# Third tile of x requested by SyncE ahead of V's weights, and a longer run of dummy matmuls ahead of the first V matmul

## The chip, the cores and the metric

The kernel runs on one core of one Trainium2 chip. The metric is the device time of one execution, in microseconds (us). The core's engines work side by side, each on its own queue of instructions in order: TensorE (PE in the profile; its weight loads are PEld), VectorE (DVE), ScalarE (ACT), GpSimd (POOL) and SyncE (SP). In this kernel SP does nothing but request transfers, and ACT requests some between its arithmetic. A request occupies the engine that makes it; the bytes are then moved by 16 DMA engines that all queues share.

## The reference

One input x of 2048 rows by 576 is normalized per row, and the normalized rows go through an attention with 32 heads of 18 and a sliding window of 256, and through a gated feed-forward layer of width 4608. Both results are added to x.

```python
xn = layernorm(x)                       # mean, variance per row, eps 1e-5
q, k, v = split(xn @ wqkv)              # 576 x 1728, 32 heads of 18
p = softmax(where(0 <= i - j < 256, q k^T * 18**-0.5, -1e9))
A = (p @ v) @ wo
B = (silu(xn @ w1) * (xn @ w3)) @ w2    # 576 x 4608, 4608 x 576
out = x + A + B
```

All tensors are bf16.

## The kernel before

The rows are handled in four chunks of 512 (`CH`), each of four tiles of 128 rows. A list of operations is built in program order by `add(engine, ...)`; afterwards `resolve` works out which semaphore waits each needs from the buffers that it reads and writes, and every engine replays its own operations in the order in which they were added. So the order of the calls is the order of every queue, and a DMA request sits in the queue of the engine that it was added to.

A chunk consists of the projections to Q, K and V (`proj_begin`, `proj_end`, `proj_part`), then 36 units of the feed-forward layer's first product (`unit_pairs`, line 768) with the attention's scores (630) and products with V (698) spread among them, and then the second product together with the output projection (`p2_mm`, line 839). Most matmuls come in pairs: one on the upper 64 rows of the TensorE array and one on the lower 64, each with its own bank of PSUM.

The change concerns the start of the first chunk, before the matrix work is under way. In program order:

- `load_x(t, eng)` (line 306) requests tile t of x, 128 x 576, into the buffer `xp`. The loop at lines 894 and 895 requests tile 0 on SP and tiles 1, 2 and 3 on ACT. Below, x0 to x3 are these tiles.
- ACT then loads an activation table (896), and SP requests V's weights: `wv` for the first 512 rows (897), then two pieces for the last 64 rows (901, "the tail of wv").
- SP goes on with the weights of Q and K into a buffer that lies in `pt` (927 and 931); POOL deals them into the tile `wp` in the order in which the projections read them (`deal`, 952).
- TensorE starts with dummy matmuls on a constant (921): three with 512 columns and 56 with 64 columns. Nothing reads their results. Two more follow behind the statistics of tile 0 (`warm`, 909).
- Layer norm of tile 0: statistics on DVE (396, 399), the square root on ACT (369), its reciprocal on DVE (374), the normalization on DVE (414). Tile 1 takes its statistics on ACT (387, 390). Tiles 2 and 3 take theirs on DVE, and the statistics of tile 2's first half stand in DVE's queue between the normalization of tile 0 and the reciprocal for tile 1.
- `xn_turn` transposes a normalized tile on TensorE (429), and ACT copies the result into `xnT` (442, 448).
- `warm_halves` (915) then issues one dummy pair on the two row halves with 256 columns into the banks that the first V projection will use, and `proj_begin(0, ("v", 0))` issues that projection: 288-column matmuls (500) with a tile of `xnT` standing and `wv` moving. Tiles 1 to 3 follow in the same manner, and the Q and K projections after them (also line 500, 512 columns, with `wp` standing).

Of the kernel before, what the change touches and what calls it, by code (L numbers as in the profile page):

```python
# [44 lines left out]
class _Prog:  # L45
# [13 lines left out]
    def add(self, eng, fn, r=(), w=(), j=(), dma=None, after=()):  # L59
        deps = []  # L60
        for k in r:
            deps += self.bufs[k].writers
        for k in w:
            g = self.bufs.get(k)
            if g is not None:
                deps += g.ahead(eng)
        for k in j:
            g = self.bufs[k].before
            if g is not None:
                deps += g.ahead(eng)  # L70
        op = _Op(eng, fn, deps + list(after), dma)
        op.after = tuple(after)
        self.n[eng] += 1
        op.pos = self.n[eng]
        if dma is not None:
            self.dma_count[dma] = self.dma_count.get(dma, 0) + 16
            op.cnt = self.dma_count[dma]
        for k in r:
            self.bufs[k].readers.append(op)
        for k in w:  # L80
            self.bufs[k] = _Gen([op], self.bufs.get(k))
        for k in j:
            self.bufs[k].writers.append(op)
        for k in w:
            if self.bufs[k].before is not None:
                self.bufs[k].before.before = None
        self.ops.append(op)
        return op
# [76 lines left out]
def bass_parallel_sum__sliding_block__glu_gated_swiglu__prompt_kernel(  # L165
# [17 lines left out]
    CH = 512  # L183
# [14 lines left out]
    with ExitStack() as es:  # L198

        def sb(name, shape, dtype=dt.bfloat16):  # L200
            return es.enter_context(nc.sbuf_tensor(name, shape, dtype))
# [66 lines left out]
        oq = sb("oq", [128, CH])  # L268
# [9 lines left out]
        PS = es.enter_context(nc.psum_tensor("ps", [128, 8, 512], dt.float32))  # L278
        JOBS, SC = ((0, 1), (2, 3), (4, 5)), (6, 7)
# [22 lines left out]
        def load_x(t, eng="sp"):  # L302
            nonlocal xp_ctr
            s = xp_ctr % NXP
            xp_ctr += 1
            add(eng, lambda e: e.dma_start(xp[s][:], x2[t * 128:(t + 1) * 128, :]), w=[("xp", s)], dma=f"xp{s}")
            return s
# [228 lines left out]
        def proj_begin(c, what, banks=None):  # L536
            banks = banks or job()
            last = proj_part(c, what, banks, 0)
            got = proj_end()
            pend.append((c, what, banks, last))  # L540
            return got
# [350 lines left out]

        xslot = {}
        for t in range(TB):
            xslot[t] = load_x(t, "act" if t else "sp")
        add("act", lambda e: e.preload_act_table_set("sqrt_and_others"))
        add("sp", lambda e: e.dma_start(
            wv[:, 0:4, :], A_wqkv[0:512, 2 * D:3 * D].rearrange("(kd p) f -> p kd f", p=128)),
# [10 lines left out]
                add("pe", lambda e, n=n: e.matmul(PS[:, b, 0:n], oq[:, 0:128], oq[:, 0:n], start=True, stop=True),  # L909
                    r=["oq0"], after=after, **{"j" if k else "w": [("ps", b)]})  # L910

        def warm_halves(banks):
            for r in range(2):
                rows = slice(64 * r, 64 * r + 64)
                add("pe", lambda e, b=banks[r], rows=rows, r=r: e.matmul(
                    PS[:, b, 0:256], oq[rows, 0:128], oq[rows, 0:256], start=True, stop=True, tile_position=(64 * r, 0)),
                    r=["oq0"], w=[("ps", banks[r])])

        ones = nc.const_aps.tensor(1.0, (128, CH), dt.bfloat16)
        for k, n in enumerate([CH] * 3 + [64] * 56):  # L920
            add("pe", lambda e, n=n: e.matmul(PS[:, 4, 0:n], ones[:, 0:128], ones[:, 0:n], start=True, stop=True),
                **{"j" if k else "w": [("ps", 4)]})

# [45 lines left out]
        ln_recip(0)  # L969
        ln_apply(0, xslot[0], (0, 2))  # L970
        xn_turn(0, (SC, JOBS[1]), ("act", "act"), spread=True)()
        warm_halves(JOBS[0])
        proj_begin(0, ("v", 0))
        ln_stats(2, xslot[2], 0)
        ln_recip(1)
# [72 lines left out]
        for c in range(NC):  # L1048
# [13 lines left out]
            start = START[c]  # L1062
# [119 lines left out]
            for u in range(NF):  # L1182
# [31 lines left out]
                if u in stat:  # L1214
                    t = (c + 1) * TB + stat[u]
# [4 lines left out]
                if u in apply:  # L1220
                    t = (c + 1) * TB + apply[u]
# [5 lines left out]
                if c == 0 and u == 13:  # L1227
                    for t in range(4):
                        r0 = 4 * Dh + 252 * (t // 2)
                        rows = A_wo[r0:r0 + 252, :].rearrange("(s p d) f -> p s d f", p=2, d=Dh)[t % 2, :, :, :]  # L1230
                        add("sp", lambda e, t=t, rows=rows: e.dma_start(wo[0:126, t, :], rows),
                            dma="wo", **{"j" if t else "w": ["wo"]})
                if c == 0 and u == 18:
                    rows = A_wo[0:4 * Dh, :].rearrange("(n d) f -> n d f", d=Dh)
# [16 lines left out]
            banks = ()  # L1251
            n = -3
            for item in p2_list(c):
# [14 lines left out]
                elif n in (100, 120) and c + 2 < NC:  # L1268
                    t = (c + 2) * TB + (n == 120)
# [34 lines left out]
```

## Time and profile before

| | |
|---|---|
| median of 3 runs | 555.33 us |
| the three runs | 555.33, 556.86, 555.22 us |
| the profiled execution's own time | 555.15 us |
| its span, from the first instruction to the last | 553.4 us |
| TensorE busy | 549.7 us, 99% of the span |
| VectorE, ScalarE, GpSimd busy | 57%, 47%, 38% of the span |

Rows of the profile that follow are read so. A row of the timeline or of the chain begins with the start in us from the beginning of the span and the duration in us; then come the engine, the line of the kernel, the operation, the tiles written and read, and the number of instructions merged into the row. A bracket gives the idle time of the engine just before the row and what ended it. A "q" behind an engine's name marks its queue: a DMA request there is the time that the request took, not that of the transfer. A row of a tile's own view ends with the shortest, median and longest duration in ns, and one line below them gives the time from request to landing for the requests of the window that was asked for. Matmuls overlap, so a matmul's duration is longer than the distance to the next.

### The profile page before, as it was taken

The numbers are of one execution on the slowest core, as the hardware profiler recorded it, in microseconds if no ns is written. First come the engines' busy times: TensorE is split into PE (matmuls) and PEld (weight loads), VectorE is DVE, ScalarE is ACT, GpSimd is POOL, SyncE is SP. The second block draws the span as 40 slices with busy tenths as digits, with TensorE's granted clock in tenths as the row PEclk, the third lists the DMA queues.
The fourth block names the chain that finished last, engine by engine and source line by source line (L and its number), as shares of the span: only waits on it lengthen the run. The fifth ranks groups of instructions, "written<-read, shape, count | busy, mean of one in ns | idle before, by whom it ended". The sixth has DMA issues, their size and how long they took to land.

```text
span 553.4 us, 18355 instructions
## 1 busy us (share of the span) xinstructions
PE 549.7 (99%) x8071; PEld 331.4 (60%) x8072; DVE 313.3 (57%) x587; ACT 259.3 (47%) x365; POOL 210.7 (38%) x380
## 2 busy tenths in 40 slices
PE   8999999999999999999999999999999999999998
PEld 6555544777555544577765454557776545445776
DVE  8476797710468886651056988655105567866311
ACT  7457776000288567700037857760005784775000
POOL 4324675400047456530005745643001553663100
PEclk9999999999999999999999999999999999999999
DMA  9997888576576953857746885466663673541750
GB/s 255 213 193 178 193 208 208 137 199 182 141 144 149 184 134 91 187 142 196 185 109 140 176 154 141 119 153 166 183 182 83 138 172 104 150 115 46 194 152 23
DMA packets 128038, 86.00 MB, mean 155 GB/s; under 512 B 35702, under 2 KB 125646, under 8 KB 127958
## 3 DMA queue, kind: packets, MB, share of 16 engines
q1 hardware_dynamic: 89138, 62.80, 48.7%
q10 hardware_dynamic: 38820, 22.02, 15.6%
q8 instruction: 63, 1.03, 0.8%
q14 instruction: 17, 0.14, 0.1%
HBM read 71.29 MB, written 2.36 MB: 133 GB/s over the span
## 4 chain that ended last, share of the span: by engine, by line
PE 98%; DMA 0%; ACT 0%; DVE 0%; issue 0%
PE ps L768 51%; PE ps L839 29%; PE ps L500 10%; PE ps L630 6%; PE ps L698 3%; DMA xp<-in_A_x_dram 0%; DVE stats L396 0%; ACT hT L390 0%; PE ps L429 0%; ACT sd L369 0%; ACT xnT L442 0%; DVE ofin L861 0%; DVE mv L399 0%
## 5 line engine op out<-in xcount | busy, mean ns | idle before, releaser
L768 PE MATMUL ps<-xnT,w 64*128 64x512 bf16 x1400 | 185.6, 376 | 0.0
L768 PE MATMUL ps<-xnS,w 64*128 64x512 bf16 x1120 | 151.7, 376 | 0.0
L839 PE MATMUL ps<-w,hT 64*128 64x288 bf16 x2292 | 143.7, 282 | 0.0
L783 DVE SCALAR_TENSOR_TENSOR gs<-th,ps 128x512 bf16<-128x512 bf16 x144 | 97.9, 680 | 78.8 <-ACT th L777 77.9
L839 PEld LDWEIGHTS ps<-w,hT 64*128 64x128 bf16 x2292 | 112.1, 94 | 29.6 <-issue 0.2
L777 ACT ACTIVATE th<-ps 128x512 bf16<-128x512 f32 x144 | 85.6, 595 | 60.6 <-PE ps L768 59.7
L768 PEld LDWEIGHTS ps<-xnT,w 64*128 64x128 bf16 x1400 | 66.7, 94 | 64.5 <-issue 0.2
L786 DVE SCALAR_TENSOR_TENSOR hT<-gs,ps 128x512 bf16<-128x512 bf16 x144 | 98.9, 687 | 5.0
L667 POOL TENSOR_TENSOR pt<-pt,mk 128x256 bf16<-128x256 bf16 (+1 forms) x143 | 85.5, 622 | 25.7 <-ACT pt L639 25.7
L639 ACT ACTIVATE pt<-ps 128x1024 bf16<-128x1024 f32 (+1 forms) x80 | 80.7, 1009 | 24.6 <-PE ps L630 24.1
L667 POOL TENSOR_TENSOR hT<-hT,mk 128x256 bf16<-128x256 bf16 (+1 forms) x52 | 30.3, 604 | 160.5 <-ACT hT L639 160.5
L768 PEld LDWEIGHTS ps<-xnS,w 64*128 64x128 bf16 x1120 | 53.1, 94 | 51.2
L513 ACT ACTIVATE stage<-ps 128x512 bf16<-128x512 f32 x16 | 9.6, 597 | 139.4 <-PE ps L500 137.1
L870 DVE TENSOR_TENSOR ofin<-ps,xp 128x288 bf16<-128x288 f32 x31 | 12.2, 451 | 98.5 <-PE ps L839 98.5
L630 PE MATMUL ps<-qv,kv 64*128 64x320 bf16 (+4 forms) x528 | 51.3, 260 | 0.0
L630 PEld LDWEIGHTS ps<-qv,kv 64*128 64x128 bf16 x528 | 25.7, 94 | 29.2 <-ACT pt L639 1.7
L500 PE MATMUL ps<-xnT,wp 64*128 64x512 bf16 (+1 forms) x360 | 38.3, 355 | 0.0
L731 DVE STREAM_TRANSPOSE od<-oq 128x256 bf16<-128x256 bf16 x64 | 25.4, 426 | 12.1 <-POOL oq L724 12.1
L639 ACT ACTIVATE hT<-ps 128x1024 bf16<-128x1024 f32 (+1 forms) x28 | 28.4, 1015 | 7.6 <-PE ps L630 7.4
L667 POOL TENSOR_TENSOR stage<-stage,mk 128x256 bf16<-128x256 bf16 (+1 forms) x44 | 24.8, 585 | 14.2 <-ACT stage L639 14.2
L639 ACT ACTIVATE stage<-ps 128x1024 bf16<-128x1024 f32 (+1 forms) x24 | 24.3, 1013 | 6.9 <-PE ps L630 6.8
L500 PEld LDWEIGHTS ps<-xnT,wp 64*128 64x128 bf16 x360 | 18.1, 94 | 14.6
(94 smaller groups left out, 394.5 us busy)
## 6 DMA issues: line engine op xcount, KB each, us to landing
w<-in_B_w_dram SPq DMA_DIRECT2D x210, 192.0 KB, 4.1
w<-in_B_w_dram ACTq DMA_DIRECT2D x70, 288.0 KB, 3.6
xp<-in_A_x_dram SPq DMA_DIRECT2D x29, 144.0 KB, 4.1
out_dram<-ofin SPq DMA_DIRECT2D x31, 72.0 KB, 1.7
xnS<-xnT SPq DMA_DIRECT2D x8, 256.0 KB, 4.7
oT<-od SPq DMA_DIRECT2D x56, 36.0 KB
pt<-in_A_wqkv_dram SPq DMA_DIRECT2D x4, 288.0 KB, 5.3
hT<-in_B_w_dram SPq DMA_DIRECT2D x6, 192.0 KB, 6.9
```

The lines of the kernel that those rows point to most:

```text
L500: op = add("pe", lambda e, out_=out_, st=st, mv=mv, n=n, r0=r0, first=first: e.matmul(out_, st, mv, start=first, stop=(part == 1 and n == ...
L630: add("pe", lambda e, r0=r0, out_=out_, kb=kb, q0=q0, nb=nb: e.matmul(out_, kb4[r0:r0 + 64, g, kb + NV - NB, :] if kb < 0 else kv[r0:r0 + ...
L639: add("act", lambda e: e.activation(pt_slot(sl)[:, :, 0:w], PS[:, SC[0]:SC[1] + 1, 0:w], ACT.Exp, scale=scale), r=[("ps", b) for b in SC], ...
L667: add("pool", lambda e, vb=vb, mm=mm: e.tensor_tensor(vb, vb, mm, ALU.mult), r=(key if n == 0 else []) + ["mk"], **{"w" if n == 0 else "j" ...
L698: add("pe", lambda e, p=p, q=q, pr=pr, sl=sl, g=g, pos=pos, q0=q0, nb=nb, col=col, first=first, n=n: e.matmul(PS[32 * q:32 * q + VW, banks ...
L731: add("dve", lambda e: e.transpose(od[i][:, g % 2, c0:c0 + CH // 2], oq[:, c0:c0 + CH // 2]), r=["oq", "oq0"], **{"j" if half or g % 2 els ...
L768: op = add("pe", lambda e, n=n, r0=r0, r=r, k=k, src=src: e.matmul(PS[:, b0 + r, :], wt[r0:r0 + 64, k, fl * 128:(fl + 1) * 128], src, star ...
L777: add("act", lambda e: e.activation(th[i][:], PS[:, bg, :], ACT.Tanh, scale=0.5), r=[("ps", bg)], w=[("th", i)])
L783: add("dve", lambda e: e.scalar_tensor_tensor(out=gs[i][:], in0=th[i][:], scalar=1.0, in1=PS[:, bg, :], op0=ALU.add, op1=ALU.mult), r=[("t ...
L786: add("dve", lambda e: e.scalar_tensor_tensor(out=hT[:, u, :], in0=gs[i][:], scalar=0.5, in1=PS[:, bu, :], op0=ALU.mult, op1=ALU.mult), r= ...
L839: op = add("pe", lambda e: e.matmul(PS[:, bank, 0:w], stat, move, start=new, stop=False, skip_group_check=True, **tile), r=keys, after=hel ...
L870: add("dve", lambda e: e.tensor_tensor(ofin[:, o, :], PS[:, bank, 0:HD], xp[xs[n]][:, d0:d0 + HD], ALU.add), r=[("ps", bank), ("xp", xs[n] ...
```

## The change

```diff
         for t in range(TB):
-            xslot[t] = load_x(t, "act" if t else "sp")
+            xslot[t] = load_x(t, ("sp", "act")[t % 2])
...
-        def warm_halves(banks):
+        def warm_halves(banks, cols):
             for r in range(2):
                 rows = slice(64 * r, 64 * r + 64)
                 add("pe", lambda e, b=banks[r], rows=rows, r=r: e.matmul(
-                    PS[:, b, 0:256], oq[rows, 0:128], oq[rows, 0:256], start=True, stop=True, tile_position=(64 * r, 0)),
+                    PS[:, b, 0:cols], oq[rows, 0:128], oq[rows, 0:cols], start=True, stop=True, tile_position=(64 * r, 0)),
                     r=["oq0"], w=[("ps", banks[r])])
...
-        for k, n in enumerate([CH] * 3 + [64] * 56):
+        for k, n in enumerate([CH] * 3 + [128] * 4 + [64] * 48):
...
-        warm_halves(JOBS[0])
+        for cols in (256, 256, 128):
+            warm_halves(JOBS[0], cols)
```

SP now requests x0, x2 and then `wv`; ACT requests x1 and x3. The first row of dummy matmuls has four with 128 columns and 48 with 64 in place of 56 with 64. Ahead of the first V projection stand three dummy pairs, with 256, 256 and 128 columns, in place of one with 256.

## The prediction

> **What bounds the kernel now.** I read the page first, then the chain of work that ended last over the first 14 us, then the busy times of the whole rest.
>
> ```profile
> span 553.4 us, 18355 instructions
> ```
>
> ```profile
> 0.79 2.70 DMA xp<-in_A_x_dram
> ...
> 4.91 0.77 ACT hT L390 x2
> ...
> 6.01 0.39 ACT xnT L442
> ...
> 6.54 0.67 PE ps L500 x8
> ...
> 7.42 1.20 PE ps L500 x18
> ...
> 10.39 3.76 PE ps L500 x45
> ```
>
> ```profile
> 10.40:552.00 541.60, 540.74 (x7925) 325.03 (x7923) 305.00 (x564) 252.25 (x345) 207.22 (x367) 1.00 0.65 154
> ```
>
> The last row gives a window, its length and then TensorE's busy time: from 10.4 us on TensorE is busy for 540.74 of 541.60 us. The change adds or removes no work there. What it can alter is when TensorE gets under way: the chain runs from x0's landing through the statistics, ScalarE's square of tile 1 (L390) and the copy to `xnT` to the first V matmul at 6.54, and from 10.39 on TensorE feeds itself. Time won or lost ahead of 6.54 counts once, and only if it is on this chain.
>
> **The change part by part.** The requests first, as the timeline has them:
>
> ```profile
> 0.79 0.40 SPq L306 DMA_DIRECT2D xp<-in_A_x_dram  x1
> 0.80 1.44 ACTq L306 DMA_DIRECT2D xp<-in_A_x_dram  x3
> 1.25 0.42 SPq L897 DMA_DIRECT2D wv<-in_A_wqkv_dram  x1
> 2.27 1.28 ACT L896 ACT_TABLE_LOAD   x1 [2.27 <-issue]
> 3.72 0.68 ACT L387 ACTIVATE hT<-xp 128x576 f32<-128x576 bf16 x1 [0.16 <-DMA xp<-in_A_x_dram]
> ```
>
> SP's first request begins at 0.79 and its second at 1.25, so an x request takes SP 0.46 us. Everything behind it on SP moves by that: `wv` is requested at 1.71 instead of 1.25, its tail and the weights of Q and K 0.46 us later each. ACT is relieved of one request, 1.44 / 3 = 0.48 us: the table load would end at 3.07 instead of 3.55. But L387 then waits for x1 until 3.72 in any case, so this buys 0; the 0.16 us of that bracket is the most it could buy if x1 came sooner too.
>
> *x2 itself.* Of the x requests begun at 0.80 and 1.24 on ACT (x1 and x2), and of DVE behind them:
>
> ```profile
> L306 ACTq DMA_DIRECT2D xp<-in_A_x_dram x2: 412/432/452, 0.8 to 1.2; - x2
> ...
> DMA to landing us min/median/max: 2.9/3.7/4.4
> ```
>
> ```profile
> 5.14 0.62 DVE L414 TENSOR_SCALAR xn<-xp,mv,rstd 128x512 bf16<-128x512 bf16 x2
> 5.68 0.45 DVE L396 BATCH_NORM_STATS2 stats<-xp 128x6 f32<-128x288 bf16 x1
> 6.05 0.14 DVE L374 RECIPROCAL rstd<-sd 128x1 f32<-128x1 f32 x1
> ```
>
> x1 lands 2.9 us after 0.80, at 3.7, x2 4.4 us after 1.24, at 5.6. Tile 2's first statistics start at 5.68, right behind tile 0's normalization and with no idle time in the row. So x2 is just in time, and an earlier x2 wins nothing, since DVE is not free sooner. In an execution in which x2 came later it would hold up tile 1's reciprocal behind it, and that the change would cure. Value taken 0, as this execution has it; bounds 0 and a gain of 0.3 us (an estimate: a landing later by two of the reciprocals, 2 x 0.14).
>
> *V's weights* now stand behind x2 on SP.
>
> ```profile
> L897 SPq DMA_DIRECT2D wv<-in_A_wqkv_dram x1: 418/418/418, 1.2 to 1.2; - x1
> ...
> DMA to landing us min/median/max: 4.6/4.6/4.6
> ```
>
> ```profile
> xp<-in_A_x_dram SPq DMA_DIRECT2D x29, 144.0 KB, 4.1
> ...
> wv<-in_A_wqkv_dram SPq DMA_DIRECT2D x1, 576.0 KB, 4.6
> ```
>
> ```profile
> 1.00:2.00 1.00, 1.00 (x3) 0.30 (x2) 0.62 (x2) 0.00 (x0) 0.77 (x6) 1.00 0.15 23
> 2.00:3.00 1.00, 1.00 (x19) 0.94 (x18) 1.00 (x1) 0.73 (x1) 0.94 (x3) 1.00 0.89 252
> 3.00:4.00 1.00, 1.00 (x24) 1.00 (x21) 0.81 (x3) 0.84 (x2) 0.99 (x2) 1.00 1.05 339
> 4.00:5.00 1.00, 1.00 (x23) 1.00 (x21) 0.60 (x3) 0.88 (x4) 0.00 (x0) 1.00 1.08 385
> 5.00:5.50 0.50, 0.28 (x6) 0.20 (x4) 0.46 (x3) 0.50 (x2) 0.00 (x0) 1.00 1.06 369
> ```
>
> `wv` lands at 1.25 + 4.6 = 5.85. The last two columns of the windows are the DMA engines' busy share and GB/s: from 2 us on they are full, so the bytes ahead decide and not the moment of a request. All four x tiles and `wv` are 4 x 144 + 576 = 1152 KB, which is 1.18 MB; by 5.5 us the engines have moved 0.023 + 0.252 + 0.339 + 0.385 + 0.185 = 1.18 MB. Even with every x tile ahead of it, `wv` is through at about 5.5, and with the lag of now (5.85 against 5.5) it lands near 5.85 again. That is the low bound. The high one passes the whole delay on: 1.71 + 4.6 = 6.31. I take 5.9, near the first, because the engines are full. The first V matmul waits for `xnT`, whose copy ends at 6.01 + 0.39 = 6.40. Both bounds lie ahead of it: 0 on the chain, with 0.09 us of cover at the high bound.
>
> *What stands behind it on SP.*
>
> ```profile
> L901 SPq DMA_DIRECT2D wv<-in_A_wqkv_dram x1: 582/582/582, 2.3 to 2.3; - x1
> ...
> DMA to landing us min/median/max: 4.5/4.5/4.5
> ```
>
> ```profile
> 10.04 3.48 POOL L952 COPY wp<-pt 128x360 f32<-128x360 f32 x8 [6.05 <-DMA pt<-in_A_wqkv_dram]
> ```
>
> ```profile
> 11.41 0.79 PEld L500 LDWEIGHTS ps<-xnT,wp 64*128 64x128 bf16 x10
> ```
>
> The later piece of `wv`'s tail lands at 2.3 + 4.5 = 6.8; delayed in full, at 7.3. The first pairs that read it are the last of V's first projection, within the row that begins at 7.42. POOL's first deal waits for the weights of Q and K until 10.04; the first Q projection needs two deals (3.48 / 8 = 0.44 us each), so its weights stand at 10.92, and TensorE loads them at 11.41. Delayed in full they stand at 11.38. Both cost 0, and again the bytes ahead of these transfers are the same as before.
>
> *The dummy matmuls.*
>
> ```profile
> 3.79 1.47 PE L921 MATMUL ps<-const-bfloat16-1.0 128*128 128x64 bf16 x24
> 5.72 0.34 PE L429 MATMUL ps<-ident,xn 64*128 64x64 bf16 x10
> 5.89 0.27 PE L915 MATMUL ps<-oq 64*128 64x256 bf16 x2
> 6.54 0.30 PE L500 MATMUL ps<-wv,xnT 64*128 64x288 bf16 x2 [0.38 <-ACT xnT L442]
> ```
>
> ```profile
> L921 PE MATMUL ps<-const-bfloat16-1.0 x59: 242/242/634, 0.8 to 5.0; 128*128 128x64 bf16 x56, 128*128 128x512 bf16 x3
> ```
>
> ```profile
> 20.98 12.95 PE ps L768 x120
> ```
>
> The 24 dummies follow each other every (1.47 - 0.24) / 23 = 0.053 us, 1.2 columns a ns; the 60 pairs of 512 columns at 20.98 go at 60 x 512 / 12950 = 2.37 columns a ns. So TensorE starts at half rate. The four V pairs at 6.54 come every (0.67 - 0.30) / 3 = 0.12 us for 288 columns, 2.3 a ns: full rate has come by then, although the granted clock in the windows says 1.00 throughout. The first row of dummies keeps its columns (56 x 64 = 4 x 128 + 48 x 64 = 3584) and so its length. If its length went by the count of instructions, it would end 4 x 0.053 = 0.21 us sooner, and TensorE would wait for tile 0 at 5.72 just the same: 0 at both bounds. The pairs ahead of V grow from 256 to 640 columns. From 5.89 they stream until 6.16 at full rate and until 6.42 at half rate, both ahead of 6.54: they fill the bracket of 0.38 us there and cost 0. If that cover were gone, the 384 columns would cost 0.16 or 0.32 us.
>
> **Sum.** Requests 0, x2 0, `wv` 0, the weights behind it 0, dummies 0. On the profiled execution's 555.15 us (its span of 553.4 and 1.75 around it) that gives 555.15; it stands 0.18 below the median of the runs, 555.33, and the fastest run, 555.22, lies between; I take 555.2.
>
> **The rivals.** *x2 was holding DVE up in most executions:* tile 1's reciprocal and all of DVE behind it come up to 0.3 us sooner. For it speaks that x2 lands within 0.1 us of its use, against it that the one trace shows no wait: 555.15 - 0.15 = 555.0 in the middle of its bounds.
>
> *V's weights come late:* the full request delay and in addition x3, now earlier on the other queue, taking its 144 KB (147 KB at 377 GB/s, the mean of the last two windows: 0.39 us) ahead of them: 6.31 + 0.39 = 6.70, 0.3 us behind `xnT`, so 555.45. It decides from a landing at 6.40 on. Against it stands the byte count.
>
> *The slower side: TensorE's full rate comes late.* The place is the V projections from 6.54 on. A pair at half rate takes 0.24 instead of 0.12 us, so half of each us that the clock lags behind 6.54 is lost; at 9.8 that is 1.6 us, which is also the distance of the run of 556.86 from the lowest, 555.22. So: 555.2 + 1.6 = 556.8, past the bound named below if full rate comes later than about 10.1. For it speaks that one run of three lies there, and that nothing in the program sets the clock; against it that the change closes part of the idle time that lies ahead of 6.54. If two runs of three fell so, it would be the median. The Trainium skill, "TensorE: Matmul & The Clock Gate", Part 1, says that the array starts at half clock and gets the full one after a busy window of some 3.4 us that runs free of the kernel, so that the moment differs from run to run; an estimate by it is a loss of 3.4 / 2 = 1.7 us in a run whose busy window is missed, 556.9, and by it the added pairs could only help. The start at half rate agrees with that (0.053 us for 64 columns); no row here shows the window.
>
> **How the numbers follow.** No effect on the chain: 0.58, at 555.2 with a range of its own of 554.9 to 555.5. x2 held DVE up: 0.12. V's weights late: 0.08. The clock late: 0.14. What I don't see: 0.08. The bound of 0.3%, about what a measurement of this kernel can tell from no change, is 1.67 us on 555.33: 553.66 and 557.0. To be faster by that, V would have to start at 6.54 - 1.67 = 4.87, ahead of ScalarE's square of tile 1 at 4.91, behind which 1.6 us of the chain still follow; so no rival reaches it, and 0.04 of the unseen stands there. Slower takes half of the late clock, 0.07, and 0.03 of the unseen. That gives 0.04, 0.86 and 0.10. The range reaches from the gain of 0.3 us, with the spread of before around it, to the late clock: 554.7 to 556.9.
>
> **What would show it.** In the changed profile x2 should land at about 4.2 (the x tiles' 0.59 MB have moved by 3.9, and the lag of 0.3 as for `wv`), `wv` at 5.85 to 6.3, with the first V matmul still released by the copy to `xnT` at about 6.40 and started at 6.54; tile 2's first statistics at 5.68; three dummy pairs between 5.9 and 6.5 with little idle time behind; V pairs every 0.12 us; POOL's first deal at 10.04 to 10.5; the same busy time behind 10.4. I am wrong if the first V matmul is released by `wv`'s transfer, if the deals hold up the first Q projection, or if V pairs still come every 0.24 us.

## The result, and the profile after

| | before | after |
|---|---|---|
| median | 555.67 us (22 runs, 555.12 to 557.3) | 556.78 us (22 runs, 555.38 to 558.65) |
| ratio | | 1.002, 95% interval 1.0011 to 1.0028 |
| profiled execution | 555.15 us, span 553.4 | 557.17 us, span 555.4 |

The changed kernel is slower by 0.2%, some 1.1 us, which is little, but the interval is clear of 1; its runs spread wider. The first rows are from its timeline, in the same form as before.

```profile
1.71 0.43 SPq L897 DMA_DIRECT2D wv<-in_A_wqkv_dram  x1
...
5.72 0.46 DVE L396 BATCH_NORM_STATS2 stats<-xp 128x6 f32<-128x288 bf16 x1
...
5.91 0.44 PE L915 MATMUL ps<-oq 64*128 64x256 bf16 x6
...
7.66 0.36 PEld L500 LDWEIGHTS ps<-wv,xnT 64*128 64x128 bf16 x8 [1.54 <-DMA wv<-in_A_wqkv_dram]
...
11.99 1.86 POOL L952 COPY wp<-pt 128x360 f32<-128x360 f32 x5 [7.99 <-DMA pt<-in_A_wqkv_dram]
...
12.93 1.25 PE L500 MATMUL ps<-xnT,wp 64*128 64x512 bf16 x10 [0.49 <-POOL wp L952]
```

V's weights are requested at 1.71, as worked out. But the first V matmul is now released by their transfer and not by the copy to `xnT`: TensorE loads them at 7.66, where before the first V matmul had started at 6.54. GpSimd's first deal of Q's weights comes at 11.99 instead of 10.04, and the first Q matmul, which waits for it, at 12.93 instead of 11.44, where the kernel before has this row:

```profile
11.44 1.25 PE L500 MATMUL ps<-xnT,wp 64*128 64x512 bf16 x10
```

From there on TensorE is as dense as before, 540.00 us of 541.10:

```profile
12.90:554.00 541.10, 540.00 (x7907) 324.46 (x7907) 303.79 (x560) 250.80 (x342) 206.77 (x365) 1.00 0.66 153
```

So 1.49 of the 2.0 us by which this span is longer are there at the first Q matmul. The other half microsecond lies scattered behind it and was not followed. The view of `wv`, for the request at 1.71, gives the transfer itself:

```profile
L897 SPq DMA_DIRECT2D wv<-in_A_wqkv_dram x1: 434/434/434, 1.7 to 1.7; - x1
...
DMA to landing us min/median/max: 5.9/5.9/5.9
```

It takes 5.9 us instead of 4.6 and lands at 7.6. Where the time went shows in windows of half a microsecond; the last two columns are the DMA engines' busy share and GB/s. First the kernel before, then the changed one.

```profile
3.50:4.00 0.50, 0.50 (x14) 0.50 (x11) 0.48 (x2) 0.34 (x2) 0.49 (x1) 1.00 1.07 378
4.00:4.50 0.50, 0.50 (x14) 0.50 (x12) 0.47 (x2) 0.49 (x2) 0.00 (x0) 1.00 1.06 378
4.50:5.00 0.50, 0.50 (x14) 0.50 (x12) 0.14 (x2) 0.39 (x2) 0.00 (x0) 1.00 1.10 392
5.00:5.50 0.50, 0.28 (x6) 0.20 (x4) 0.46 (x3) 0.50 (x2) 0.00 (x0) 1.00 1.06 369
```

```profile
3.50:4.00 0.50, 0.50 (x14) 0.50 (x11) 0.43 (x2) 0.24 (x1) 0.50 (x1) 1.00 0.99 346
4.00:4.50 0.50, 0.50 (x14) 0.50 (x12) 0.47 (x3) 0.50 (x2) 0.00 (x1) 1.00 1.09 323
4.50:5.00 0.50, 0.50 (x14) 0.50 (x12) 0.14 (x2) 0.37 (x3) 0.00 (x0) 1.00 1.01 318
5.00:5.50 0.50, 0.47 (x7) 0.13 (x4) 0.46 (x2) 0.50 (x1) 0.00 (x0) 1.00 0.94 311
```

In these 2 us the engines moved (378 + 378 + 392 + 369) / 2 = 758 KB before and 649 KB after, 14% less. A packet is one record of the DMA trace, here a row of 1152 bytes that takes 0.051 us as a rule; the 109 KB that are missing are 95 packets, 4.8 us of one engine's time. The busy share fell by 6% only, from a mean of 1.07 to 1.01. So less than half of the loss is idle time of the engines, and the rest lies in packets that took long: six in these 2 us took over 0.2 us, 2.86 us together, where the kernel before has one, of 0.22 us.

A transfer raises its semaphore once for each of its 16 engines, and for V's main weights 13 of the 16 come by 6.16, the last three at 7.46, 7.60 and 7.62. So three engines are about 1.5 us behind. The semaphores do not name them, but the transfers that follow in the queue have as many late ends: the last of the pieces that the first deal needs lands at 11.86, two microseconds later than before.

Two theories come from this. A: the later requests of the weights cost the time (A1 or M: the moment of the request; A2 or O: the order and the bytes ahead). B: the dummy matmuls cost it. Later two more were added: T, the first reads of an untouched region of memory are slow; and R, the DMA engines run empty because the next bytes were requested too late. Q and S stand for what the expectations of e6 and e9 say of them.

### The profile page after: what moved, and what is told of

Same layout as the page of the kernel before. It is cut to its first block, busy times and chain, and to the rows that moved or that the text cites. A ratio compares the mean times of both kernels' runs of the same rounds, so it can differ in the third digit from the quotient of the medians.

```text
span 555.4 us, 18356 instructions
## 1 busy us (share of the span) xinstructions
PE 550.1 (99%) x8072; PEld 331.7 (60%) x8072; DVE 313.5 (56%) x587; ACT 259.3 (47%) x365; POOL 210.8 (38%) x380
## 4 chain that ended last, share of the span: by engine, by line
PE 97%; DMA 1%; SPq 1%; issue 0%; POOL 0%; DVE 0%; POOLq 0%
PE ps L768 51%; PE ps L839 29%; PE ps L500 9%; PE ps L630 6%; PE ps L698 3%; DMA pt<-in_A_wqkv_dram 1%; SPq L901 0%; SPq L927 0%; POOL wp L952 0%; SPq L306 0%; SPq L931 0%; SPq L897 0%; DVE ofin L861 0%; POOLq L154 0%
## 5 line engine op out<-in xcount | busy, mean ns | idle before, releaser
L870 DVE TENSOR_TENSOR ofin<-ps,xp 128x288 bf16<-128x288 f32 x31 | 12.2, 451 | 98.5 <-PE ps L839 98.5
```

The source lines that it names most:

```text
L870: add("dve", lambda e: e.tensor_tensor(ofin[:, o, :], PS[:, bank, 0:HD], xp[xs[n]][:, d0:d0 + HD], ALU.add), r=[("ps", bank), ("xp", xs[n] ...
```

## The experiments

Each edit is against the kernel before; the indented texts are what was expected ahead of the runs. For each kernel the table has one traced execution, in us: when V's main weights were requested and their first packet, their 13th and their last engine's end as the trace's semaphores have them, the first V and the first Q matmul; then the ratio to the kernel before with its 95% interval. A dash stands where the requests of V's weights are not told apart. The ratio comes from all runs, and one traced execution need not be typical of them: e9's is the fastest of its 11 runs, e7's the slowest of its 12.

```
kernel                request first  13th  last | first V first Q | ratio   interval
before                   1.25  2.97  5.63  5.82 |  6.54   11.44   |
changed                  1.71  3.71  6.16  7.62 |  7.67   12.93   | 1.0020  1.0011 to 1.0028
e1 x2 only               1.71  3.71  7.05  7.90 |  7.95   12.84   | 1.0025  1.0013 to 1.0037
e2 dummies only          1.25  2.94  5.77  6.12 |  6.59   12.07   | 1.0006  0.9997 to 1.0015
e3 small request ahead   1.71  3.39  6.55  8.09 |  8.14   14.14   | 1.0040  1.0025 to 1.0056
e4 x2 and x3 on SP       2.19  4.24  7.64  8.01 |  8.05   14.16   | 1.0039  1.0024 to 1.0054
e5 V's weights delayed   1.80  3.79  7.32  7.78 |  7.83   13.94   | 1.0040  1.0025 to 1.0054
e6 V's weights on ACT    1.24  3.30  5.66  5.79 |  6.57   11.59   | 0.9999  0.9990 to 1.0008
e7 meant: x3 late        1.71  3.90  6.12  7.77 |  7.82   13.93   | 1.0030  1.0015 to 1.0045
e8 early touch           1.72  3.75  6.23  7.51 |  7.56   13.56   | 1.0026  1.0015 to 1.0037
e10 e6 + dummies         1.24  3.22  5.64  5.86 |  6.44   11.46   | 0.9996  0.9985 to 1.0007
e11 e6 + tail on ACT     1.24  3.20  5.53  5.66 |  6.42   11.44   | 1.0000  0.9985 to 1.0016
e9 four requests, SP     1.70  3.72    -   6.43 |  6.58   11.82   | 1.0030  1.0020 to 1.0040
e12 four, two queues     1.70    -     -   7.09 |  7.14   12.02   | 1.0009  0.9998 to 1.0019
```

**The two halves of the change, e1 and e2.** The request order alone, and the dummies alone:

```diff
 e1
-            xslot[t] = load_x(t, "act" if t else "sp")
+            xslot[t] = load_x(t, ("sp", "act")[t % 2])
 e2
-        for k, n in enumerate([CH] * 3 + [64] * 56):
+        for k, n in enumerate([CH] * 3 + [128] * 4 + [64] * 48):
...
-        warm_halves(JOBS[0])
+        for cols in (256, 256, 128):
+            warm_halves(JOBS[0], cols)
```

> The kernel before with the request order alone (x2 on SP ahead of V's weights), dummies as before. Theory A (the later requests of V's and Q's weights cost it): as slow as the changed kernel, ratio 1.001 to 1.003, with V's main weights or Q's weights landing later than TensorE wants them (first V matmul after 6.6 or first Q matmul after 11.6). Theory B (the dummy matmuls cost it): 0.999 to 1.0007.

> The kernel before with the dummy matmuls alone. Theory A: 0.999 to 1.0007, first V matmul at 6.5, first Q matmul at 11.4. Theory B: ratio 1.001 to 1.003.

The request order alone gives 1.0025, as much as the whole change; the dummies' interval holds 1. Theory B falls. e2's trace shows something else besides. In its timeline:

```profile
6.30 0.46 DVE L396 BATCH_NORM_STATS2 stats<-xp 128x6 f32<-128x288 bf16 x1 [0.42 <-DMA xp<-in_A_x_dram]
```

There, with the old request order, x2 did land late, at 6.28, and DVE waited 0.42 us for it. The wait that the change takes away is real, in that execution at least.

**Moment or bytes, e3 and e4.** e3 puts a request of 128 rows of 32 bytes between x0 and V's weights and leaves x2 on ACT; e4 puts x3 on SP too.

```diff
 e3
+        add("sp", lambda e: e.dma_start(scrap[:, :], x2[0:128, 0:16]), w=["scrap"], dma="scrap")
         add("sp", lambda e: e.dma_start(
             wv[:, 0:4, :], A_wqkv[0:512, 2 * D:3 * D].rearrange("(kd p) f -> p kd f", p=128)),
...
 e4
-            xslot[t] = load_x(t, "act" if t else "sp")
+            xslot[t] = load_x(t, "act" if t == 1 else "sp")
```

> The kernel before with one more request on SP between x0 and V's weights: 128 rows of 32 bytes, so about as long to request as a tile of x, with a thirty-sixth of its bytes; x2 stays on ACT. Theory A1 (the moment of the request decides): as slow as the changed kernel, ratio 1.001 to 1.003. Theory A2 (the bytes ahead decide): 0.999 to 1.0007.

> x2 and x3 on SP ahead of V's weights, x1 alone on ACT, dummies as before. Theory A1 (moment of the request): V's weights are requested at 2.17, twice the delay, ratio 1.003 to 1.006. Theory A2 (bytes ahead): all x tiles are ahead of them anyway, as the changed kernel, 1.001 to 1.003. Theory B: 0.999 to 1.0007.

With almost no bytes moved ahead, e3 is slow (1.004): that speaks for A1 and against A2. All 128 packets of x3 came there behind 4.0 us, with V's weights on their way since 3.39, so the engines had something else to move; and the rate from 3.5 to 5.5 us never fell below that of this window:

```profile
4.50:5.00 0.50, 0.50 (x14) 0.50 (x12) 0.20 (x1) 0.35 (x3) 0.00 (x0) 1.00 0.92 295
```

e4, with twice the delay, has 1.0039, no more than e3 with the single one; that twice the delay costs more is not shown. e3 adds 128 small packets of its own, though, so the moment had to be tried with no request added.

**The moment alone, e5, and V's weights early with x2 early, e6.** e5 makes the request of V's weights wait for a memset on GpSimd, and with it all that stands behind on SP, about half a microsecond; it changes nothing else. e6 requests x0, x2, x3 on SP and x1, then V's main weights, on ACT.

```diff
 e5
-            add("pool", lambda e, i=i: e.memset(xn[i][:, D:640], 0.0), w=[("xnd", i)])
+            cleared = add("pool", lambda e, i=i: e.memset(xn[i][:, D:640], 0.0), w=[("xnd", i)])
...
-            w=["wv"], dma="wv")
+            w=["wv"], after=(cleared,), dma="wv")
 e6
-        for t in range(TB):
-            xslot[t] = load_x(t, "act" if t else "sp")
+        for t in range(2):
+            xslot[t] = load_x(t, ("sp", "act")[t])
+        add("act", lambda e: e.dma_start(
+            wv[:, 0:4, :], A_wqkv[0:512, 2 * D:3 * D].rearrange("(kd p) f -> p kd f", p=128)),
+            w=["wv"], dma="wv")
+        for t in range(2, TB):
+            xslot[t] = load_x(t, "sp")
...
-        add("sp", lambda e: e.dma_start(
-            wv[:, 0:4, :], A_wqkv[0:512, 2 * D:3 * D].rearrange("(kd p) f -> p kd f", p=128)),
-            w=["wv"], dma="wv")
```

> The kernel before, x requests as before (x0 on SP; x1, x2, x3 on ACT), with V's main weights requested only behind GpSimd's second memset of xn, at about 1.75 instead of 1.25; no request is added or moved to another queue. Theory M (the later moment of the request is enough): ratio 1.001 to 1.004, with packets of V's weights that take over 0.4 us and a last landing after 6.6. Theory O (it is the order, x2's and x3's packets being gone when V's weights start, so that an engine that waits for a slow first read has nothing else to move): x3 is still behind x2 on the other queue and fills in, ratio 0.999 to 1.001.

> x0, x2, x3 on SP, x1 and then V's main weights on ACT, so that V's weights are requested at 1.24 as in the kernel before, while x2 comes as early as in the changed kernel and the weights of V's tail, of Q and of K are requested 0.46 us later than before. Theory M: V's weights land by 6.4 and the ratio is 0.999 to 1.001. Theory O: the same, since x2 and x3 fill in. Theory Q (the weights of Q and K, requested later, cost the time, and V's do not): 1.001 to 1.004 with the first V matmul at 6.5 and the first Q matmul after 11.8.

e5's timeline, then its windows:

```profile
1.80 0.40 SPq L897 DMA_DIRECT2D wv<-in_A_wqkv_dram  x1
...
7.82 0.36 PEld L500 LDWEIGHTS ps<-wv,xnT 64*128 64x128 bf16 x8 [1.82 <-DMA wv<-in_A_wqkv_dram]
...
11.90 1.87 POOL L952 COPY wp<-pt 128x360 f32<-128x360 f32 x5 [7.89 <-DMA pt<-in_A_wqkv_dram]
```

```profile
3.50:4.00 0.50, 0.50 (x13) 0.50 (x11) 0.41 (x2) 0.23 (x1) 0.50 (x1) 1.00 0.84 263
4.00:4.50 0.50, 0.50 (x14) 0.50 (x12) 0.47 (x3) 0.50 (x2) 0.01 (x1) 1.00 0.81 131
4.50:5.00 0.50, 0.50 (x14) 0.50 (x12) 0.15 (x1) 0.36 (x3) 0.00 (x0) 1.00 0.77 205
5.00:5.50 0.50, 0.32 (x6) 0.20 (x4) 0.45 (x2) 0.50 (x1) 0.00 (x0) 1.00 0.94 295
```

And e6's:

```profile
1.24 0.45 ACTq L896 DMA_DIRECT2D wv<-in_A_wqkv_dram  x1
...
6.54 0.39 PEld L500 LDWEIGHTS ps<-wv,xnT 64*128 64x128 bf16 x8 [0.45 <-issue]
...
9.99 3.46 POOL L954 COPY wp<-pt 128x360 f32<-128x360 f32 x8 [5.99 <-DMA pt<-in_A_wqkv_dram]
```

```profile
3.50:4.00 0.50, 0.50 (x20) 0.50 (x17) 0.33 (x1) 0.16 (x1) 0.50 (x1) 1.00 1.04 362
4.00:4.50 0.50, 0.50 (x20) 0.49 (x16) 0.49 (x2) 0.50 (x2) 0.00 (x1) 1.00 1.10 399
4.50:5.00 0.50, 0.11 (x4) 0.11 (x2) 0.21 (x1) 0.35 (x4) 0.00 (x0) 1.00 1.10 392
```

This pair settles that the moment of the request decides. e5 moves no x tile and is slow; its engines fall to 131 GB/s between 4 and 4.5. e6 moves x2 ahead as the change does, requests Q's and K's weights 0.48 us later than before, as the changed kernel does, and costs nothing, with V's weights requested at 1.24: the engines stay at 362 to 399 GB/s and the first deal comes at 9.99. Theories A2 and Q fall. O does not fall by e5, since only 34 of x3's 128 packets were left there after 4.0; against it stands e3, where all were left and the cost was the same.

The pair also says how late is too late. In e5 SP's queue moves no data between x0's last packet at 3.17 and the first of V's weights at 3.79, which is 2.0 us after their request; x0, a request of a quarter of the rows, shows its first packet at 1.83, 1.0 us after its request. The x tiles are nearly through at 4 us, so a request at 1.7 to 1.8 starts to deliver only as they run out. That is theory R.

R is not the whole of it. In the hole between 4 and 4.5 e5's engines are busy for 0.81 of their time and move 131 GB/s, where the kernel before has 1.06 and 378: the bytes fall by two thirds, the busy time by a quarter. Packets of up to 0.73 us make up most of the difference. Idle engines and slow packets come together in the slow kernels, and no run here tells which brings the other. Nor does the depth of the hole set the cost: e3 never fell below 295 GB/s and costs as much as e5.

**Two other explanations, e7 and e8.** e7 was to hold x3 back behind ACT's table load, so that its packets fill in; e8 reads 32 bytes of every fourth row of V's columns on GpSimd's queue at the start. Both have the changed request order and the old dummies.

```diff
 e7
         for t in range(TB):
-            xslot[t] = load_x(t, "act" if t else "sp")
-        add("act", lambda e: e.preload_act_table_set("sqrt_and_others"))
+            if t == 3:
+                add("act", lambda e: e.preload_act_table_set("sqrt_and_others"))
+            xslot[t] = load_x(t, ("sp", "act")[t % 2])
 e8
+        add("pool", lambda e: e.dma_start(
+            scrap[:, :], A_wqkv[0:512, 2 * D:2 * D + 16].rearrange("(p four) f -> p four f", four=4)[:, 0, :]), w=["scrap"], dma="scrap")
```

> The changed request order (dummies as before) with x3 requested behind ACT's table load, so that its packets still wait when V's weights start. Theory O: the lag of the slowest engines shrinks, ratio under 1.0015. Theory M: as the changed kernel, 1.001 to 1.004.

> The changed request order (dummies as before) with a small read by GpSimd's queue at the very start, of 32 bytes from every fourth row of V's columns of the weights. Theory T (the slow packets are the first reads of a region of memory that nothing has read yet): no packet of V's weights over 0.4 us, the first V matmul at 6.5, ratio 0.999 to 1.001. Theories M and O: as the changed kernel, 1.001 to 1.004.

e7 did not do what it says. ACT's timeline:

```profile
1.24 1.28 ACT L896 ACT_TABLE_LOAD   x1 [1.24 <-PEq L1290]
1.27 0.42 ACTq L306 DMA_DIRECT2D xp<-in_A_x_dram  x1
```

The request goes out 0.03 us into the table load, so e7 is one more measurement of the changed order (1.003). In e8 the touch landed only at 4.71, with V's weights already on their way, so it hardly came first; packets of up to 0.48 us remain and the last engine ends at 7.51. T is not borne out, and not excluded.

**R by itself, e9 and e12.** V's main weights in four requests of 128 rows, with x2 ahead of them: all on SP (e9), or the first on SP and three on ACT behind x3 (e12).

```diff
 e9
-        add("sp", lambda e: e.dma_start(
-            wv[:, 0:4, :], A_wqkv[0:512, 2 * D:3 * D].rearrange("(kd p) f -> p kd f", p=128)),
-            w=["wv"], dma="wv")
+        for kd in range(4):
+            add("sp", lambda e, kd=kd: e.dma_start(
+                wv[:, kd, :], A_wqkv[128 * kd:128 * kd + 128, 2 * D:3 * D]), dma="wv", **{"j" if kd else "w": ["wv"]})
 e12
+            add("act" if kd else "sp", lambda e, kd=kd: e.dma_start(
...
```

> The changed request order (dummies as before) with V's main weights in four requests of 128 rows each instead of one of 512. Theory R (a request of 512 rows shows its first packet 1.7 to 2.05 us after it begins, one of 128 rows after 1.04 us, and the DMA engines run empty in between because the x tiles are through at 3.7 to 4): the first packet of V's weights comes right behind the last of x2, few engines are empty between 3.5 and 5, V's weights land by 6.4, ratio 0.999 to 1.0012 although the weights of Q and K are requested 1.4 us later still. Theory S (the reads of these rows are slow however they are requested): as the changed order, ratio 1.001 to 1.004 or more.

> The changed request order of x (x2 on SP behind x0, x3 on ACT behind x1; dummies as before) with V's main weights in four requests of 128 rows, the first on SP behind x2 and the other three on ACT behind x3, so that SP requests the weights of Q and K when the changed kernel does. Theory R (an engine runs empty where the next bytes are requested too late, and that is the whole cost): no window between 3.5 and 7 under 300 GB/s, first V matmul at 6.5, first deal at about 10, ratio 0.999 to 1.001. If x2 ahead of V's weights costs by itself, however they are requested: 1.0015 to 1.004.

e9's timeline and windows:

```profile
6.55 0.39 PEld L500 LDWEIGHTS ps<-wv,xnT 64*128 64x128 bf16 x8 [0.49 <-DMA wv<-in_A_wqkv_dram]
...
10.88 1.86 POOL L952 COPY wp<-pt 128x360 f32<-128x360 f32 x5 [6.89 <-DMA pt<-in_A_wqkv_dram]
```

```profile
4.00:4.50 0.50, 0.50 (x14) 0.50 (x12) 0.47 (x2) 0.42 (x2) 0.00 (x0) 1.00 1.14 380
...
5.50:6.00 0.50, 0.50 (x14) 0.28 (x12) 0.50 (x4) 0.41 (x3) 0.00 (x0) 1.00 0.72 123
6.00:6.50 0.50, 0.38 (x10) 0.06 (x4) 0.46 (x3) 0.45 (x2) 0.00 (x0) 1.00 0.59 77
6.50:7.00 0.50, 0.42 (x8) 0.37 (x10) 0.47 (x2) 0.49 (x3) 0.00 (x0) 1.00 0.69 175
```

Half of what R expected came. The hole at 4 us is gone (380 GB/s), V's weights land at 6.43 and TensorE loads them at 6.55. But SP, busy with three more requests, asks for the weights of Q and K 1.4 us later, and now the hole is there: 123, 77 and 175 GB/s from 5.5 to 7, with a busy share of 0.59 to 0.72 and packets of up to 0.97 us. In both places the rate fell where the next bytes were asked for late. The first deal slips to 10.88, and the ratio stays at 1.003, which is what S expected and not R. The trace does not account for this ratio: it is of an execution 0.9 us under the median of e9's runs, and its first Q matmul is only 0.38 us late.

e12 spreads the requests over both queues and has its ratio down to 1.0009, with an interval that holds 1 but also overlaps that of e1. Its traced execution does not bear R out. Two of its windows:

```profile
3.50:4.00 0.50, 0.50 (x13) 0.50 (x11) 0.40 (x2) 0.50 (x1) 0.49 (x1) 1.00 1.20 367
...
6.50:7.00 0.50, 0.15 (x4) 0.00 (x0) 0.46 (x3) 0.50 (x4) 0.00 (x0) 1.00 1.10 277
```

The engines are full throughout, and 277 GB/s is the lowest rate from 3.5 to 7, where R expected 300. Still V starts at 7.14 and not at 6.5, and the first deal comes at 11.08 and not at 10. One packet of 1.22 us stands at 3.63, in a window of 367 GB/s. So slow packets can come without a hole, R alone is not the whole cost, and how much of it belongs to either stays open.

**A version with all of it, e10 and e11.** e10 is e6 with the changed dummies; e11 is e6 with the tail of V's weights on ACT as well.

```diff
 e11
-            add("sp", lambda e, p=p: e.dma_start(
+            add("act", lambda e, p=p: e.dma_start(
                 wv[64 * p:64 * p + 64, 4, (1 - p) * HD:(2 - p) * HD],
...
```

> V's main weights on ACT at 1.24, x2 and x3 on SP, with the changed kernel's dummy matmuls. If the dummies are harmless by themselves: ratio 0.999 to 1.0008, as the same order without them (0.9999). If they cost something: 1.0005 to 1.0015.

> As the kernel with V's main weights on ACT, and the two pieces of their tail on ACT as well, so that SP requests the weights of Q and K 0.8 us sooner than before. If the DMA engines are full from there on (theory R's other half): no gain, ratio 0.999 to 1.0008, first deal at about 10. If the moment of these requests mattered too: first deal before 9.6 and a ratio under 0.9995.

e10 does both things that the change says, x2 early and more dummies, and is even with the kernel before: 0.9996, 0.9985 to 1.0007. e11's first deal comes at 9.75 and its ratio is 1.0000; Q's and K's weights are not short of an earlier request. No version tried beats the kernel before by more than can be measured.

## Why the prediction was wrong

**The step that failed** is the one on V's weights: "I take 5.9, near the first, because the engines are full", with 6.31 as the high bound. The premise "from 2 us on they are full, so the bytes ahead decide and not the moment of a request" was read from a trace in which V's weights are requested at 1.25. It holds for that request and is no property of the engines. Requested at 1.71, the same bytes met engines that were in part idle and in part held up by slow packets (14% fewer bytes from 3.5 to 5.5), and the landing was 7.6, 1.3 us past the bound that was to pass the whole delay on; a request that comes 0.46 us later does not land 0.46 us later. That the moment decides is shown by e5 and e6; by which way a late request loses so much is not. "Both cost 0, and again the bytes ahead of these transfers are the same as before" fell with it: the first deal's weights landed 2.0 us later, with late ends in every transfer in between. Two of the prediction's own signs of being wrong came: the first V matmul was released by `wv`'s transfer, and the deals held up the first Q projection.

**The rival "V's weights come late"** had the right place and, with "against it stands the byte count", the wrong argument. It was priced at 0.3 us; the first V matmul moved by 1.13 in the changed kernel's trace and by 1.41 in e1's, the median by 1.1. Its reason for the loss, x3's 147 KB ahead of V's weights, is not the one either: e5 leaves x3 where it was and is slow. It was the case that came true, with a chance of 0.08.

**x2.** It landed at 4.23, where I had put 4.2, and tile 2's statistics started at 5.72, with DVE never waiting for it. The rival "x2 was holding DVE up" is true of one traced execution (0.42 us in e2), but what its cure is worth cannot be told from nothing in e6 and e10.

**The dummies** cost 0, as said: e2's and e10's intervals hold 1. The three pairs lie between 5.91 and 6.35, ahead of the first V matmul.

**The clock late.** It did not come about as foreseen: the changed kernel's V matmuls run at full rate from the start, the first eight in 0.66 us as before in 0.67. In other versions a drop of the clock appears behind the first V matmul, as a second loss. Windows of e5:

```profile
5.37:8.79 3.42, 1.71 (x35) 1.09 (x36) 3.33 (x13) 2.13 (x9) 0.00 (x0) 1.00 1.09 320
...
6.00:7.80 1.80, 0.21 (x4) 0.01 (x2) 1.73 (x7) 1.33 (x6) 0.00 (x0) 1.00 1.05 326
...
8.80:12.20 3.40, 3.40 (x40) 2.21 (x36) 1.72 (x5) 2.10 (x8) 0.30 (x1) 0.50 1.15 252
```

While V's weights are awaited TensorE is busy for 0.21 of 1.80 us, and from 8.8 to 12.2 the granted clock is 0.50. That stretch from the first V to the first Q matmul then takes 6.11 us instead of 4.90. The same drop stands in the traces of e3, e4, e7 and e8, not in those of the changed kernel and e1. V's first matmul is about equally late in e1 and e5, by 1.41 and 1.29 us, but Q's by 1.40 and 2.50. So the drop can add another microsecond. Whether it is also part of how widely such kernels' runs spread was not traced. The Trainium skill ("TensorE: Matmul & The Clock Gate", Part 1) has the clock fall to half after an idle window of about 3.4 us; the length of the drop agrees, 3.4 us here, but no such window was idle: of the 3.42 us ahead of the drop, which the trace's clock record has as its first stretch at full rate, TensorE was busy for 1.71. In e3, e4, e7 and e8 the same stretch holds 1.32 to 1.71 us of work. In e1 the first 3.41 us of that record hold 1.95, and no drop follows:

```profile
6.49:9.90 3.41, 1.95 (x44) 1.59 (x46) 2.35 (x11) 2.10 (x9) 0.00 (x0) 1.00 1.12 302
```

**The sign and the size.** No effect on the chain was the likeliest case, at 0.58, and that did not hold: the interval of the ratio lies above 1. The loss of 0.2% is under the bound of 0.3% and 556.78 lies inside the range, whose upper end the clock case had set for a different reason; that it lies inside is luck.

## What to carry to other kernels

A queue that looks full in a profile may be full because its requests came in time. Before a request is moved back, look for how long ahead of its first packet it was made (here 1.0 us for x0's 128 rows, and 1.7 us in the kernel before to 2.0 us in e5 for the 512 rows of V) and whether the bytes ahead of it last that long. When several queues can issue, put the large request on the queue where it goes out soonest and let the small ones queue up behind each other, as e6 does. A wait at the start of a TensorE-bound kernel can cost more than its length, because the clock may drop behind it: in e5 the first V matmul is 1.29 us late and the first Q matmul 2.50.

## What the runs showed of the hardware that was not expected

- The engines do not fall behind together. In the changed kernel 13 of 16 finish V's main weights by 6.16 us and three at 7.46 to 7.62, and a lag stays with later transfers (the last of the deal's pieces: most engines by 9.77, the last six between 10.81 and 11.86). Single packets of 1152 bytes, 0.051 us as a rule, take up to 0.81 us there, and 1.36 us in e1. In e1 the ends are spread: eight of 16 by 6.05, the others from 6.65 to 7.90. Why some engines only, and why these reads are slow, stays open.
- A table load on ScalarE does not hold up a DMA request behind it: in e7 the request went out 0.03 us into a load of 1.28 us. So what a request occupies is the engine's queue, and the unit that computes can be at work meanwhile.
- e3 and e5, where the requests of V's weights and of all behind them come late and no x tile is moved, cost more by their ratios (1.004) than the change itself (1.002), though the intervals still touch, from 1.0025 to 1.0028. Their traces have the drop of the clock and those of the changed kernel and e1 do not, which may be the reason; no run separates it.
